# First unit of a retention and two-layer FFN kernel: the activation's sum kept in its PSUM bank, and five decoding operations issued earlier

## The chip, the cores and the metric

The kernel runs on one core of one Trainium2 chip. The time is the device time of one execution in microseconds; the median of several runs is compared.

## The reference, cut to what matters

```python
def reference(**kwargs):
    attn_out = _attn_ref(**attn_kwargs)              # retention: 4 batches, 8 heads, 768 steps, 64 per head
    x = attn_out.transpose(0, 2, 1, 3).reshape(B * S, H * D)     # 3072 tokens x 512
    x = _moe_ref(x=x, **moe_kwargs)
    return _moe2_ref(x=x, **moe2_kwargs)             # gated experts, one per token

def _moe_ref(x, w_in, w_out):
    h = x @ w_in                                     # 512 -> 2048
    g = np.maximum(h, 0.0) + np.log1p(np.exp(-np.abs(h)))
    return (g @ w_out).astype(np.float32)            # 2048 -> 512
```

The change lies in the second of the three parts, in the computation of `g`.

## The kernel before, in words

The 3072 tokens are worked on in 8 units of 384 tokens. Unit T of the feed-forward layer and the retention of unit T+1 run in one pipeline of 16 steps, one for each slice `f` of 128 of the 2048 hidden columns; steps are counted through, s = 16 T + f. Step s issues, in this order on each engine (the order is written out by hand in the loop over `s`, and each engine runs its queue in that order):

- a piece of the retention of the next unit (`attn_a`, `attn_m`: two small products and two masks `am`),
- `dec`: some operations of the decoding of the weights (below),
- `mm1(s)`, line 621: 12 matmuls of the first layer into a PSUM bank `hp`. These banks come from a pool of two, so the bank of step s is that of step s-2,
- in six steps of the first unit (2, 3, 5, 6, 8, 9) the transposes `tq` and their copy `kt` or `qt` on ScalarE (`attn_prep`, line 430),
- `act_a(s)` on ScalarE: `u` = |h| (line 632), `u` = exp(-u) (633), in the first unit `t` twice (635, 636), `ln` = log(1+u) (637), which with `t` makes a corrected log1p,
- the rest of the retention piece (`attn_b`: sums `y`, state update `wsb` on VectorE),
- `dec_fin`: for each decoded weight block the copy of its high half on ScalarE (line 340), the load of a further block, and its low half on GpSimd (342),
- `act_p(s)` on GpSimd (VectorE for the very first): two additions that finish `ln` (648, 649),
- `act_hi(s-1)`: the sum `g` on VectorE (659 in the first unit), then its rounded high half `hi` on ScalarE (660),
- one more decoding operation, then `act_lo(s-1)`: the low half `lo` = g - hi on VectorE (666), and `dec_fin` again,
- `mm2(s-2)`, line 678: 9 matmuls of the second layer with `hi` and `lo` of step s-2.

The matmuls run on operands split into a high and a low half, so every matrix product is made of three.

The weights of the feed-forward layer come as 64-bit floats. They are decoded during the first unit, in 32 blocks, each with three VectorE operations (lines 321, 325, 329: mask and shift, or, or), 96 in all; `dec(n)` issues the next n of them. 30 are issued in the opening before step 0, the rest in the steps: before the change 2 in step 0, one in step 1, and then by turns four and five a step up to step 15. A block `m` has two buffers.

The line of the loop that sets this, and the place of the sum:

```python
                dec(3+s%2 if s > 1 else (2, 0)[s])
                ...
                    dec(1 if s > 1 else 1)
```

After the feed-forward part come the gate, the sorting of tokens to experts and the experts' layers; they are untouched.

Of the kernel before, what the change touches and what calls it, by code (L numbers as in the profile page):

```python
# [7 lines left out]
F32 = mybir.dt.float32  # L8
# [4 lines left out]
ALU = mybir.AluOpType  # L13
# [8 lines left out]
TT = 384  # L22
# [53 lines left out]
def retention_moe_moe2(ctx: ExitStack, tc: tile.TileContext, a: dict, out: bass.AP):  # L76
    nc = tc.nc
# [200 lines left out]
    with tc.manual_schedule():  # L278
        with ExitStack() as p1:
# [5 lines left out]
            gp2 = p1.enter_context(tc.tile_pool(name="gp2", bufs=2))  # L285
# [58 lines left out]
            def dec(n):  # L344
                for _ in range(n):
                    next(steps, None)
# [60 lines left out]
            def attn_scale_q(U, p):  # L407
                if U < UN:
                    scale_nat(U, p, st[U, p]["qs"], qnat)
                    return  # L410
                qs = st[U, p]["qs"].rearrange("p (c j) -> p c j", j=32)
                r0 = U % 2 * (TT // 32)
                nc.gpsimd.tensor_tensor(
                    out=qs, in0=qs, in1=qtab[:, p, r0:r0 + TT // 32].unsqueeze(2).to_broadcast([128, TT // 32, 32]),
                    op=ALU.mult,
                )
# [17 lines left out]
            def attn_a(U, p, c, dst=None, am=None):  # L434
                s = st[U, p]
                cs = slice(c * 128, (c + 1) * 128)
                if dst is None:
                    sc = ps_s.tile([128, 512], F32, name="sc")
                    dst = (sc[:, 0:128], wps[:, 256:384])
                    am = at1.tile([128, 256], F32, name="am")  # L440
                for h in range(2):
                    hs = slice(h * 64, (h + 1) * 64)
                    nc.tensor.matmul(dst[h], lhsT=s["kt"][hs, cs], rhs=s["qt"][hs, cs], start=True, stop=True)  # L443
                s["am", c] = am, dst

            def attn_m(U, p, c):
                s = st[U, p]
                am, dst = s["am", c]
                for h in range(2):
                    i = nc.vector.tensor_tensor(out=am[:, h * 128:(h + 1) * 128], in0=dst[h], in1=mask, op=ALU.mult)  # L450
                return i
# [44 lines left out]
            def attn_first(U, i):  # L496
                if i == 0:
                    attn_load_qk(U, 0)
                    attn_load_v(U, 0)
                    attn_load_k(U, 0)  # L500
                elif i == 1:
                    attn_scale_q(U, 0)
                    attn_scale_v(U, 0)
                elif i == 2:
                    attn_prep(U, 0, 0)
                elif i == 3:
                    attn_prep(U, 0, 1)
                    attn_load_qk(U, 1)
                    attn_load_v(U, 1)

            def attn_ahead(U, i):
                p, c = seq[i]
                if c == 0 and p + 1 < NP:
                    attn_prep(U, p + 1, 0)
                if c == 1 and p + 1 < NP:
                    attn_prep(U, p + 1, 1)
# [99 lines left out]
            def mm1(T, f):  # L616
                hp = ps_h.tile([128, 512], F32, name="hp")[:, 0:TT]
                n = 0
                for w, x in ((0, xth[T]), (1, xth[T]), (0, xtl[T])):
                    for kk in range(KD):  # L620
                        nc.tensor.matmul(  # L621
                            hp, lhsT=wi[:, f, w, kk, :], rhs=x[:, kk, :], start=(n == 0), stop=(n == 3 * KD - 1),
                        )
                        n += 1
                gl[T, f] = hp

            def act_a(T, f):
                hp = gl[T, f]
                u = gp2.tile([128, TT], F32, name="u")
                ln = gp2.tile([128, TT], F32, name="ln")  # L630
                t = at1.tile([128, TT], F32, name="t")
                nc.scalar.activation(out=u, in_=hp, func=AF.Abs)  # L632
                nc.scalar.activation(out=u, in_=u, func=AF.Exp, scale=-1.0)  # L633
                if T == 0:
                    nc.scalar.activation(out=t, in_=u, func=AF.Identity, bias=1.0)
                    nc.scalar.activation(out=t, in_=t, func=AF.Identity, bias=io8[:, 7:8])
                nc.scalar.activation(out=ln, in_=u, func=AF.Ln, bias=1.0)  # L637
                g = gp2.tile([128, TT], F32, name="g")
                if T:
                    nc.scalar.activation(out=g, in_=hp, func=AF.Relu)  # L640
                gl[T, f] = u, ln, t, g, hp
# [10 lines left out]
            def act_hi(T, f):  # L652
                g, ln, hp = gl[T, f]
                hi = gp3.tile([128, TT], F32R, name="hi")
                gl[T, f] = g, ln
                if T:
                    nc.vector.tensor_tensor(out=g, in0=g, in1=ln, op=ALU.add)  # L657
                else:
                    nc.vector.scalar_tensor_tensor(out=g, in0=hp, scalar=0.0, in1=ln, op0=ALU.max, op1=ALU.add)  # L659
                nc.scalar.activation(out=hi, in_=g, func=AF.Copy)  # L660
                gh[T, f] = hi

# [146 lines left out]
            def init_records():  # L809
                rec0 = mp.tile([128, RW, 2], I32, name="rec0", tag="m")  # L810
                nc.gpsimd.memset(rec0, 0)
                nc.gpsimd.memset(rec0[:, :, 0:1], BIG)
                nc.sync.dma_start(
                    out=recd.rearrange("(p n) two -> p (n two)", p=128), in_=rec0.rearrange("p n two -> p (n two)"),
                )
# [14 lines left out]
            def zero(tiles):  # L830
                for t in tiles:
                    nc.scalar.activation(
                        out=t.rearrange("p (k t) -> p k t", k=KD), in_=ident.unsqueeze(1).to_broadcast([128, KD, 128]), func=AF.Copy, scale=0.0,
                    )
# [16 lines left out]
            for s in range(NS + 2):  # L851
                T, f = divmod(s, NF)
                U = T + 1
                i = f - 2 if U < NU and 2 <= f < 2 + len(seq) else None
                if f >= 14 and U + 1 < NU:
                    attn_first(U + 1, f - 14)
                if s == 2 * NF:
                    init_records()
                if s == 1:
                    attn_a(U, *seq[0])  # L860
                    attn_m(U, *seq[0])
                if i is not None:
                    if s != 2:
                        attn_a(U, *seq[i])
                        attn_m(U, *seq[i])
                    if i % CPU == 0 and i + CPU < len(seq):
                        attn_scale_q(U, i // CPU + 1)
                dec(3+s%2 if s > 1 else (2, 0)[s])
                if s < NS:
                    mm1(T, f)  # L870
                for fn in todo.get(s + 0.5, []):
                    fn()
                if f < 2 and 1 < U < NU:
                    attn_first(U, 2 + f)
                if i is not None:
                    attn_ahead(U, i)
                if s < NS:
                    act_a(T, f)
                if i is not None:
                    attn_b(U, *seq[i])  # L880
                dec_fin()
                if s < NS:
                    act_p(T, f)
                if s == NS:
                    hp2.extend(
                        pool.tile([128, GRP], F32, name=f"hp2_{i}", tag=tag)
                        for i, (pool, tag) in enumerate(((ps_s, "wps"), (ps_s, "y"), (ps_h, "hp"), (ps_h, "hp")))
                    )
                    lg = ps_s.tile([128, 512], F32, name="lg", tag="sc")
                    zero([lg])  # L890
                if 1 <= s <= NS:
                    act_hi(*divmod(s - 1, NF))
                    dec(1 if s > 1 else 1)
                    act_lo(*divmod(s - 1, NF))
                dec_fin()
                if i is not None:
                    attn_third(U, i)
                if s >= 2:
                    mm2(*divmod(s - 2, NF))
                if f == 1 and T > 0:  # L900
                    x1_out(T - 1)
                for fn in todo.get(s, []):
                    fn()
                if s == NS:
                    begin()
# [16 lines left out]
        with ExitStack() as left:  # L922
# [194 lines left out]
            for m, (ns, nb) in enumerate(PAIRS):  # L1117
                s, b = vis[ns], vis[nb]
# [48 lines left out]
            with tc.For_i(0, nv, 1) as it:  # L1167
                s = {"n": 0, "nb": 4, "xg": xgb[0]}
# [39 lines left out]
```

## Time and profile before

| | us |
|---|---|
| median of 3 runs | 1016.39 (1016.14 to 1019.01) |
| profiled execution, its own time | 1017.94 |
| span of its trace | 1016.1 |
| TensorE busy in the span | 962.1 (95%) |
| VectorE busy | 589.9 (58%) |
| ScalarE busy | 492.1 (48%) |
| GpSimd busy | 562.1 (55%) |

The shares are means over stages of different kinds. The slices of the span (a digit is the busy share of a fortieth in tenths) show which engine is full in which stage. The first unit takes from about 44 to 154 us. In the views, PE is TensorE, DVE is VectorE, ACT is ScalarE, POOL is GpSimd; "L659" is line 659 of the kernel. A row of the timeline gives start, duration, engine, line, operation, output and input, and in brackets the engine's idle time before it with what released it. Rows that follow each other on one engine overlap a little, so the distance of two starts is the better measure of what an operation costs in a row.

### The profile page before, as it was taken

The page shows a single profiled execution, that of the slowest core. Times are in us where ns is not written, and L with a number is a line of the kernel's source. Part 1 is how long each engine was busy: PE and PEld are TensorE (multiplying, and loading weights), DVE is VectorE, ACT ScalarE, POOL GpSimd, SP SyncE. Part 2 cuts the span into 40 slices and gives each one's busy share as a digit, 9 for nine tenths or more (in the row PEclk, how much of TensorE's full clock was granted, in tenths as well). Part 3 has the DMA queues.
Part 4 walks back from the last instruction along what each step waited for, and adds up shares of the span by engine and source line. Part 5 has one row for each costly group of instructions (what it writes and reads, how often), then busy time and mean ns, then how long its engine had stood idle before and what let it go on. Part 6 is the DMA issues. An engine that isn't in the chain of part 4 may idle for free.

```text
span 1016.1 us, 16219 instructions
## 1 busy us (share of the span) xinstructions
PE 962.1 (95%) x5666; PEld 801.4 (79%) x5666; DVE 589.9 (58%) x1292; ACT 492.1 (48%) x947; POOL 562.1 (55%) x457
## 2 busy tenths in 40 slices
PE   7798989999999999999999999999797999999994
PEld 6676768888888888888888888888685878798883
DVE  6799995546444654644564464446335375556743
ACT  3556555445445544544554454455453365354650
POOL 5577776446554653654564465446562673546642
PEclk9999999999999999999999999999897999999998
DMA  9744334123320412321041232001027394557710
GB/s 229 193 127 129 123 94 117 33 40 90 63 39 9 120 30 40 96 54 32 13 121 25 40 100 49 9 2 63 1 86 267 95 340 149 202 173 239 251 54 21
DMA packets 180692, 100.46 MB, mean 99 GB/s; under 512 B 140594, under 2 KB 159186, under 8 KB 180608
## 3 DMA queue, kind: packets, MB, share of 16 engines
q1 hardware_dynamic: 176032, 89.56, 32.0%
q0 software_dynamic: 4144, 9.04, 2.6%
q8 instruction: 46, 0.75, 0.3%
q10 hardware_dynamic: 432, 0.79, 0.2%
q14 instruction: 38, 0.31, 0.1%
HBM read 83.43 MB, written 17.85 MB: 100 GB/s over the span
## 4 chain that ended last, share of the span: by engine, by line
PE 72%; DVE 15%; issue 4%; ACT 4%; POOL 2%; DMA 2%; SPq 0%; DVEq 0%; POOLq 0%; ACTq 0%
PE hp L621 21%; PE ac L678 21%; PE op L1007 9%; PE hp L967 9%; DVE m L325 3%; PE sc L443 3%; PE y L465 3%; DVE lo L666 3%; PE hp L981 2%; DVE m L329 2%; DVE m L321 1%; PE y L463 1%; PE tp L703 1%; PE hp L179 1%; ACT hi L660 1%
## 5 line engine op out<-in xcount | busy, mean ns | idle before, releaser
L648 POOL TENSOR_TENSOR ln<-ln,t 128x384 f32<-128x384 f32 x127 | 151.3, 1191 | 260.0 <-ACT ln L637 234.5
L678 PE MATMUL ac<-wo,hi 128*128 128x512 f32 x768 | 272.4, 409 | 6.1 <-ACT hi L660 6.1
L621 PE MATMUL hp<-xth,wi 128*128 128x384 f32 x1024 | 214.8, 352 | 10.9 <-DVE g L659 10.0
L621 PEld LDWEIGHTS hp<-xth,wi 128*128 128x128 f32 x1024 | 177.7, 190 | 25.3 <-DVE g L659 11.8
L678 PEld LDWEIGHTS ac<-wo,hi 128*128 128x128 f32 x768 | 145.0, 189 | 43.4 <-ACT hi L660 7.2
L632 ACT ACTIVATE u<-hp 128x384 f32<-128x384 f32 x128 | 62.7, 490 | 240.0 <-PE hp L621 226.0
L649 POOL TENSOR_TENSOR ln<-ln,u 128x384 f32<-128x384 f32 x127 | 153.0, 1205 | 10.0
L678 PE MATMUL ac<-wo,lo 128*128 128x512 f32 x384 | 152.3, 397 | 1.1 <-DVE lo L666 0.6
L666 DVE TENSOR_TENSOR lo<-g,hi 128x384 fp32r<-128x384 f32 x128 | 97.6, 763 | 69.7 <-ACT hi L660 69.7
L621 PE MATMUL hp<-xtl,wi 128*128 128x384 f32 x512 | 110.6, 337 | 0.0
L163 POOL TENSOR_TENSOR l<-raw,h 128x1024 fp32r<-128x1024 f32 x30 | 77.1, 2580 | 54.8 <-ACT h L160 32.6
L646 DVE TENSOR_SCALAR t<-u 128x384 f32<-128x384 f32 x112 | 41.8, 373 | 95.7 <-ACT u L633 93.5
L621 PEld LDWEIGHTS hp<-xtl,wi 128*128 128x128 f32 x512 | 91.8, 190 | 0.0
L678 PEld LDWEIGHTS ac<-wo,lo 128*128 128x128 f32 x384 | 72.8, 190 | 16.3 <-DVE lo L666 4.8
L163 DVE TENSOR_TENSOR l<-raw,h 128x1024 fp32r<-128x1024 f32 x42 | 77.0, 1860 | 14.4 <-ACT h L160 14.4
L660 ACT ACTIVATE hi<-g 128x384 fp32r<-128x384 f32 x128 | 67.2, 525 | 28.6 <-DVE g L657 20.3
L482 DVE TENSOR_TENSOR wsb<-wps,wsb 64x64 f32<-64x64 f32 x112 | 24.7, 220 | 94.5 <-PE wps L474 93.8
L160 ACT ACTIVATE h<-raw 128x1024 fp32r<-128x1024 f32 x71 | 72.8, 1057 | 9.9 <-PE hp L981 3.7
L633 ACT ACTIVATE u<-u 128x384 f32<-128x384 f32 x128 | 67.2, 525 | 4.1
L637 ACT ACTIVATE ln<-u 128x384 f32<-128x384 f32 x128 | 67.1, 524 | 3.5
L657 DVE TENSOR_TENSOR g<-g,ln 128x384 f32<-128x384 f32 x112 | 61.7, 551 | 0.9 <-POOL ln L649 0.9
L1007 PE MATMUL op<-h,gh 128*128 128x512 f32 x152 | 60.0, 394 | 0.0
(218 smaller groups left out, 1578.6 us busy)
## 6 DMA issues: line engine op xcount, KB each, us to landing
raw<-in_moe_w SPq DMA_DIRECT2D x72, 512.0 KB, 5.1
raw<-in_moe_w_in SPq DMA_DIRECT2D x16, 512.0 KB, 4.0
raw<-in_moe_w_out SPq DMA_DIRECT2D x16, 512.0 KB, 3.5
kn<-in_k SPq DMA_DIRECT2D x56, 96.0 KB, 2.5
vn<-in_v SPq DMA_DIRECT2D x56, 96.0 KB, 2.6
x1d<-x SPq DMA_DIRECT2D x21, 256.0 KB, 3.1
out<-x SPq DMA_DIRECT2D x21, 256.0 KB, 3.3
ks<-in_k SPq DMA_DIRECT2D x96, 48.0 KB, 2.4
```

Source lines behind the costliest of these rows:

```text
L160: nc.scalar.activation(out=h, in_=r, func=AF.Copy)
L163: eng.tensor_tensor(out=lo, in0=r, in1=h.bitcast(F32), op=ALU.subtract)
L621: nc.tensor.matmul(hp, lhsT=wi[:, f, w, kk, :], rhs=x[:, kk, :], start=(n == 0), stop=(n == 3 * KD - 1),)
L633: nc.scalar.activation(out=u, in_=u, func=AF.Exp, scale=-1.0)
L637: nc.scalar.activation(out=ln, in_=u, func=AF.Ln, bias=1.0)
L648: eng.tensor_tensor(out=ln, in0=ln, in1=t, op=ALU.subtract)
L649: eng.tensor_tensor(out=ln, in0=ln, in1=u, op=ALU.add)
L660: nc.scalar.activation(out=hi, in_=g, func=AF.Copy)
L666: nc.vector.tensor_tensor(out=lo, in0=g, in1=gh[T, f].bitcast(F32), op=ALU.subtract)
L678: nc.tensor.matmul(ac[T, j], lhsT=x[:, js], rhs=wo[:, f, w, :], start=(f == 0 and n == 0), stop=(f == NF - 1 and n == 2),)
L967: nc.tensor.matmul(hp2[(2 * i + g) % 4][:, 0:w], lhsT=wt[:, kk, g * 128:(g + 1) * 128], rhs=x[:, kk, 0:w], start=(n == 0 and kk == 0), sto ...
L1007: nc.tensor.matmul(op, lhsT=s[x][:, f, js], rhs=s[w, f // 2][:, f % 2, :], start=(f == 0 and n == 0), stop=(f == NF2 - 1 and n == 2),)
```

## The change

In the first unit (`T` = 0) no separate buffer holds the sum `g`: VectorE writes it back into the bank `hp` that it read, and both `hi` (ScalarE) and `lo` (VectorE) read it from there. Only the units after the first keep the buffer in SBUF. Besides, step 0 issues five decoding operations ahead instead of two, and step 1 two instead of none; the steps from 2 on are issued the same numbers, so the decoding ends with step 14 instead of 15.

```diff
@@ -635,7 +635,7 @@
                 nc.scalar.activation(out=ln, in_=u, func=AF.Ln, bias=1.0)
-                g = gp2.tile([128, TT], F32, name="g")
+                g = gp2.tile([128, TT], F32, name="g") if T else hp
                 if T:
                     nc.scalar.activation(out=g, in_=hp, func=AF.Relu)
                 gl[T, f] = u, ln, t, g, hp
@@ -656,7 +656,7 @@
                 if T:
                     nc.vector.tensor_tensor(out=g, in0=g, in1=ln, op=ALU.add)
                 else:
-                    nc.vector.scalar_tensor_tensor(out=g, in0=hp, scalar=0.0, in1=ln, op0=ALU.max, op1=ALU.add)
+                    nc.vector.scalar_tensor_tensor(out=g, in0=g, scalar=0.0, in1=ln, op0=ALU.max, op1=ALU.add)
                 nc.scalar.activation(out=hi, in_=g, func=AF.Copy)
                 gh[T, f] = hi
@@ -865,7 +865,7 @@
-                dec(3+s%2 if s > 1 else (2, 0)[s])
+                dec(3+s%2 if s > 1 else (5, 2)[s])
                 if s < NS:
                     mm1(T, f)
```

VectorE's queue in steps 0 and 1, from the first operation of a decoded block to `lo` of step 0; `am` are the masks, `m` the decoded block, L648 and L649 finish `ln` of step 0. Before:

```order
L321 TENSOR_SCALAR m<-raw 128x512
L325 SCALAR_TENSOR_TENSOR m<-raw,m 128x512
L648 TENSOR_TENSOR ln<-ln,t 128x384
L649 TENSOR_TENSOR ln<-ln,u 128x384
L450 TENSOR_TENSOR am<-sc,cst 128x128
L450 TENSOR_TENSOR am<-wps,cst 128x128
L659 SCALAR_TENSOR_TENSOR g<-hp,ln 128x384
L329 SCALAR_TENSOR_TENSOR m<-raw,m 128x512
L666 TENSOR_TENSOR lo<-g,hi 128x384
```

The same place in the changed kernel, from the three operations added in step 0 on:

```order
L329 SCALAR_TENSOR_TENSOR m<-raw,m 128x512
L321 TENSOR_SCALAR m<-raw 128x512
L325 SCALAR_TENSOR_TENSOR m<-raw,m 128x512
L648 TENSOR_TENSOR ln<-ln,t 128x384
L649 TENSOR_TENSOR ln<-ln,u 128x384
L450 TENSOR_TENSOR am<-sc,cst 128x128
L450 TENSOR_TENSOR am<-wps,cst 128x128
L329 SCALAR_TENSOR_TENSOR m<-raw,m 128x512
L321 TENSOR_SCALAR m<-raw 128x512
L659 SCALAR_TENSOR_TENSOR hp<-hp,ln 128x384
L325 SCALAR_TENSOR_TENSOR m<-raw,m 128x512
L666 TENSOR_TENSOR lo<-hp,hi 128x384
```

Three operations more stand ahead of L648, and two more between the masks and the sum; the sum now goes to `hp`, and `lo` reads `hp`.

ScalarE's queue in the changed kernel, from the end of one step's chain to the end of the next one's, in the middle of the first unit (`wi` and `wo` are decoded blocks' high halves):

```order
L637 ACTIVATE ln<-u 128x384
L340 ACTIVATE wi<-m 128x512
L660 ACTIVATE hi<-hp 128x384
L340 ACTIVATE wo<-m 128x512
L632 ACTIVATE u<-hp 128x384
L633 ACTIVATE u<-u 128x384
L635 ACTIVATE t<-u 128x384
L636 ACTIVATE t<-t,cst 128x384
L637 ACTIVATE ln<-u 128x384
L340 ACTIVATE wi<-m 128x512
L660 ACTIVATE hi<-hp 128x384
```

Before, the row of `hi` read `hi<-g`; its place behind the chain of the following step is the same. In every step up to 14 exactly one block's copy stands between `ln` and `hi`; in step 15 none does any more.

VectorE's queue at the end of the first unit, from the decoding of step 15 to the first transpose for the next unit. Before:

```order
L325 SCALAR_TENSOR_TENSOR m<-raw,m 128x512
L329 SCALAR_TENSOR_TENSOR m<-raw,m 128x512
L321 TENSOR_SCALAR m<-raw 128x512
L325 SCALAR_TENSOR_TENSOR m<-raw,m 128x512
L659 SCALAR_TENSOR_TENSOR g<-hp,ln 128x384
L329 SCALAR_TENSOR_TENSOR m<-raw,m 128x512
L666 TENSOR_TENSOR lo<-g,hi 128x384
L432 STREAM_TRANSPOSE kt<-ks 128x384
```

And in the changed kernel, with step 14's end ahead of it:

```order
L659 SCALAR_TENSOR_TENSOR hp<-hp,ln 128x384
L329 SCALAR_TENSOR_TENSOR m<-raw,m 128x512
L666 TENSOR_TENSOR lo<-hp,hi 128x384
L659 SCALAR_TENSOR_TENSOR hp<-hp,ln 128x384
L666 TENSOR_TENSOR lo<-hp,hi 128x384
L432 STREAM_TRANSPOSE kt<-ks 128x384
```

The five operations of step 15 are gone: its sum follows `lo` of the step before directly.

## Rows read from the trace of the kernel before

**Rows 1.** The page's slices of the span, 40 of 25.4 us.
```profile
DVE  6799995546444654644564464446335375556743
PEclk9999999999999999999999999999897999999998
```
**Rows 2.** Busy time by stretch: length, PE, PEld, DVE, ACT, POOL, clock, DMA share, GB/s.
```profile
175.00:200.00 25.00, 25.00 (x153) 20.34 (x152) 13.88 (x37) 10.95 (x23) 13.82 (x13) 1.00 0.23 45
```
**Rows 3.** Timeline, steps 15 to 17: first-layer matmuls, ScalarE's `u` and `hi`.
```profile
142.25 2.44 PE L621 MATMUL hp<-xth,wi 128*128 128x384 f32 x8 [2.03 <-DVE g L659]
...
149.64 1.66 PE L621 MATMUL hp<-xth,wi 128*128 128x384 f32 x8 [1.43 <-DVE g L659]
...
154.52 1.57 PE L621 MATMUL hp<-xth,wi 128*128 128x384 f32 x8
...
146.07 0.49 ACT L632 ACTIVATE u<-hp 128x384 f32<-128x384 f32 x1 [3.35 <-PE hp L621]
...
152.09 0.49 ACT L632 ACTIVATE u<-hp 128x384 f32<-128x384 f32 x1 [0.20 <-PE hp L621]
...
154.11 0.53 ACT L660 ACTIVATE hi<-g 128x384 fp32r<-128x384 f32 x1
```
**Rows 4.** Timeline of TensorE: the first-layer matmuls of steps 2 and 3.
```profile
50.37 2.73 PE L621 MATMUL hp<-xth,wi 128*128 128x384 f32 x8 [2.62 <-DVE g L659]
...
57.95 1.68 PE L621 MATMUL hp<-xth,wi 128*128 128x384 f32 x8
```
**Rows 5.** Busy time by stretch, from step 2's first-layer matmuls to step 15's.
```profile
50.37:142.25 91.88, 81.30 (x439) 64.64 (x440) 88.09 (x127) 55.58 (x111) 67.29 (x51) 0.98 0.44 127
```
**Rows 6.** By line, 50 to 152 us: count, ns min/median/max, first and last start.
```profile
L666 DVE TENSOR_TENSOR lo<-g,hi x15: 1056/1366/1372, 51.3 to 151.1; 128x384 fp32r<-128x384 f32 x15
...
L490 DVE TENSOR_TENSOR xtl<-y,xth x4: 543/544/546, 74.2 to 138.0; 128x384 fp32r<-128x384 f32 x4
```
**Rows 7.** Timeline of VectorE: `lo` of step 15, after the decoding.
```profile
154.67 0.56 DVE L666 TENSOR_TENSOR lo<-g,hi 128x384 fp32r<-128x384 f32 x1 [0.59 <-ACT hi L660]
```
**Rows 8.** Timeline of VectorE, steps 0 to 2.
```profile
45.42 0.69 DVE L325 SCALAR_TENSOR_TENSOR m<-raw,m 128x512 int32<-128x512 int32 x1
48.30 0.56 DVE L648 TENSOR_TENSOR ln<-ln,t 128x384 f32<-128x384 f32 x1 [2.18 <-ACT ln L637]
...
49.77 0.55 DVE L659 SCALAR_TENSOR_TENSOR g<-hp,ln 128x384 f32<-128x384 f32 x1
...
58.73 1.33 DVE L666 TENSOR_TENSOR lo<-g,hi 128x384 fp32r<-128x384 f32 x1 [1.05 <-ACT hi L660]
```
**Rows 9.** Timeline, step 7: first-layer matmuls, and ScalarE's first operation behind them.
```profile
87.00 1.68 PE L621 MATMUL hp<-xth,wi 128*128 128x384 f32 x8
...
89.47 0.49 ACT L632 ACTIVATE u<-hp 128x384 f32<-128x384 f32 x1 [1.97 <-PE hp L621]
```
**Rows 10.** Timeline of ScalarE, step 2: first `u`, the block's copy, `hi`.
```profile
55.04 0.48 ACT L632 ACTIVATE u<-hp 128x384 f32<-128x384 f32 x1
...
57.67 0.61 ACT L340 ACTIVATE wo<-m 128x512 fp32r<-128x512 f32 x1
58.19 0.51 ACT L660 ACTIVATE hi<-g 128x384 fp32r<-128x384 f32 x1
```
**Rows 11.** Timeline, step 9, which prepares the next head pair: matmuls, ScalarE's `u`.
```profile
101.52 1.66 PE L621 MATMUL hp<-xth,wi 128*128 128x384 f32 x8
...
104.63 0.49 ACT L632 ACTIVATE u<-hp 128x384 f32<-128x384 f32 x1
```
**Rows 12.** By line, 50 to 152 us, as rows 6: the three decoding operations.
```profile
L321 DVE TENSOR_SCALAR m<-raw x21: 410/420/1427, 52.2 to 146.8; 128x512 int32<-128x512 int32 x21
...
L325 DVE SCALAR_TENSOR_TENSOR m<-raw,m x21: 676/1099/1672, 53.5 to 147.9; 128x512 int32<-128x512 int32 x21
...
L329 DVE SCALAR_TENSOR_TENSOR m<-raw,m x22: 682/1338/1719, 50.2 to 149.5; 128x512 int32<-128x512 int32 x22
```
**Rows 13.** Timeline of GpSimd: the low half of the block decoded before step 0.
```profile
45.79 1.48 POOL L342 TENSOR_TENSOR wo<-m,wo 128x512 fp32r<-128x512 f32 x1 [2.15 <-ACT wo L340]
```

## Prediction

> **What bounds the kernel now.** I read the slices of the span first. In the slices of the first unit (about 44 to 154 us) VectorE is the engine at nine tenths, and the TensorE clock dips twice [rows 1]. Later the roles change: from 175 to 200 us TensorE is busy 25.00 of 25.00 us [rows 2]. So a microsecond lost or won in the first unit arrives at the end of the kernel unchanged, because behind it stands only TensorE work without gaps. The whole question is when the first-layer matmuls of step 17 (second unit, second step) start: 154.52 us now [rows 3].
>
> Inside the first unit I looked at where the step s starts its first-layer matmuls, which I call M(s): M(2) = 50.37, M(3) = 57.95, M(15) = 142.25, M(16) = 149.64, M(17) = 154.52 [rows 3, 4]. Between M(2) and M(15), 13 steps, VectorE is busy 88.09 of 91.88 us [rows 5]: its own sum sets the pace now. M(2) waited 2.62 us for the sum `g` of step 0, so the PSUM bank is already a link of the chain [rows 4].
>
> **What the change does to each operation.** The low half `lo` reads its first input from PSUM instead of SBUF. It takes 1.366 us in the median of 15 now; the nearest row is the same operation in the same shape with one PSUM input, the split of the attention output, 0.544 us in the same stretch, narrowly spread although GpSimd works beside it [rows 6]. I take 0.54, 0.82 less. The upper end is no gain. Alone, behind the decoding, `lo` from SBUF takes 0.56 us [rows 7], so PSUM as a source costs nothing here. [...] Writing `g` to PSUM is not shown in the trace; I take its 0.55 us as it is [rows 8], with zero to 0.1 us more per step as bounds. The high half `hi` on ScalarE, now read from PSUM, is taken unchanged.
>
> The wait is the other side. The first-layer bank has two buffers, so M(s) waits until the bank of step s-2 was read for the last time. That was `g`; now it is `lo`. Between the two stand, on VectorE, one decoding operation, and on ScalarE the copy `hi`. And `hi` of step s-1 is queued on ScalarE behind the whole chain of step s (`u`, `u`, `t`, `t`, `ln`) and one decoded block's copy. That chain reads the matmuls of step s. So a **ring** closes, one turn per step: `lo`(s-2) frees the bank, the matmuls M(s) run, ScalarE does its chain, the block copy, `hi`(s-1), then `lo`(s-1), which frees the next bank. Before, `g` did not wait for `hi`, and the ring was open.
>
> **The price of one turn**, from starts of instructions: VectorE's last reader to M, 0.60 (49.77 to 50.37) [rows 4, 8]; M to `u`, 2.47 (87.00 to 89.47) [rows 9]; `u` to the block copy, 2.63, copy to `hi`, 0.52 (55.04, 57.67, 58.19) [rows 10]; `hi` to `lo`, 0.54 (58.19 to 58.73) [rows 8, 10]. Sum 6.76 us. In steps that prepare the next head pair (s = 2, 3, 5, 6, 8, 9) the transposes and one more ScalarE copy stand between M and `u`: 3.11 (101.52 to 104.63) [rows 11], so 7.40 us. A turn at the low clock, as at M(2): M to `u` 4.67, sum 8.96 [rows 4, 10].
>
> VectorE's own sum falls to (88.09 - 13 x 0.82) / 13 = 5.96 us a step [rows 5, 6]. Steps alternate between four and five decoding operations, about 0.95 us each (mean of the three medians [rows 12]), so 5.5 and 6.4 us: below the ring in every step. What `lo` saves on VectorE becomes waiting.
>
> **The start.** Three of the five moved decoding operations go ahead of the sum of step 0, into a pause: VectorE ends at 46.11 and continues at 48.30 [rows 8]. L329 runs there beside a GpSimd operation until 47.27 [rows 13], so 1.34, then 0.42 and 0.69 [rows 12]: end 48.55, 0.25 too late. Then as now 1.47 us until the place of `g` (48.30 to 49.77), 50.0; but there the other two (1.34 and 0.42) come first: `g` at 51.8. Behind it 0.55 and one more operation, 1.10, then `lo` at 53.4, and 0.60 later M(2) = **54.0**, 3.6 later than now. With the shortest durations of these rows it is 52.7, with the longest 55.4.
>
> **The sum.** M(2) 54.0. Step 2 at the low clock, since TensorE idles longer before it than now: 8.96. Steps 3 to 14: 5 x 7.40 + 7 x 6.76 = 84.3 (now 84.3: by chance the same). Step 15 has no decoding any more, its five operations went to the start, so no block copy: 6.24; but TensorE waits about 2 us before it, as at 142.25, where 2.03 us of waiting went with the low clock and M to `u` took 3.82 instead of 2.47 [rows 3, 9]: 7.59. Step 16 is of the second unit, its ScalarE chain 2.02 (152.09 to 154.11) [rows 3]: 0.60 + 2.47 + 2.02 + 0.54 = 5.63. M(17) = 54.0 + 8.96 + 84.3 + 7.59 + 5.63 = 160.5, against 154.52: **6.0 us later**. By the profiled execution, 1017.94 + 6.0 = 1023.9; that one lies 1.55 above the median of the runs, so 1016.4 + 6.0 = **1022.4 us**. What is late next: behind M(17) nothing waits for VectorE, so the loss stays.
>
> Lower end of this case: M(2) at 52.7, full clock in steps 2 and 15 (7.40 and 6.24): 156.3, 1.8 us later, 1018.2. Upper end: M(2) at 55.4, 0.1 us for `g` in each of 15 steps, one more low-clock turn (1.35): 164.7, 10.2 later, 1026.6.
>
> **Rivals.**
> *VectorE's sum stays the pace, and the kernel is faster.* Place: steps 2 to 16. If the turn is shorter than VectorE's 5.5 to 6.4 us, 15 x 0.82 = 12.3 us are won, and the five operations leave step 15 (4.8 us), less the 3.6 at the start: 13.5 faster, 1003. It decides when a turn falls below about 6.4 us, that is 0.4 below mine. For it: VectorE is the full engine now. Against it: every link of the ring is a row, and they add up to the observed 58.73 at step 2.
> *The two cancel.* The ring's links overlap a little (ScalarE starts on the bank before I think, or the decoding hides wholly in the start) and the clock stays up: the lower end above less 0.1 a step, 1016.7. For it: steps 3 to 14 come out equal anyway.
> *More low clock.* With a pause of TensorE in each turn, the low clock could hold in four more turns, 1.35 each: 5.4 more, 1028. Before, pauses of 1.43 us passed without it [rows 3], and TensorE's mean pause from M(2) to M(15), (91.88 - 81.30) / 13 = 0.81 us [rows 5], stays as it is where the steps keep their length; that speaks against it. [...]
> *`lo` does not get faster*, since `hi` still comes from SBUF beside GpSimd: each turn 0.82 longer, 15 turns, 12.3 more: 1035. The attention's split speaks against it.
>
> **Chances.** Forecast 0.60 (up to its bounds, 1019.4 to 1026.6); faster by VectorE's sum, wholly or in part, 0.11; cancelled 0.15; more low clock 0.10; no gain in `lo` 0.04. A measurement of this kernel can tell about 0.3%, 3 us, from no change. So faster 0.11, same 0.15, slower 0.74. The range 1015 to 1029 leaves out the first and the last rival and a little of the edges.
>
> **What the changed profile would show.** M(2) near 54 with a wait on `lo`, at the low clock; first-layer matmuls waiting for L666 instead of L659 in every step, starts some 6.8 and 7.4 us apart; `lo` at 0.55 us; VectorE no longer full in the first unit, waiting for `hi`; M(17) near 160. The forecast is wrong if M(3) to M(15) takes under 80 us, or if M(2) is below 52.

## The result and the profile after

The change makes the kernel slower: 1029.87 us median of 4 runs (1027.13 to 1030.99), against 1016.62 (1016.14 to 1019.01) for the kernel before on the same chip. The ratio is 1.0122 [1.0096, 1.0148], 12 us; the medians lie 13.25 us apart. The profiled execution took 1030.41 us, its span is 1028.6. The forecast had the sign and the ring, but only about half of the size (1022.4), and 1029.87 lies just outside its range.

First the page of the changed kernel: its slices and the group of the first-layer matmuls (busy us, mean ns, idle time before with what ended most of it).

```profile
DVE  5888884545644654554475464545435375556743
PEclk9989999999999999999999999999897999999998
...
L621 PE MATMUL hp<-xth,wi 128*128 128x384 f32 x1024 | 217.9, 355 | 28.3 <-DVE lo L666 28.1
```

VectorE stands at eight tenths in the first unit where it stood at nine [rows 1], so it now waits for something; and of the 28.3 us that TensorE waits ahead of a first-layer matmul, 28.1 are ended by `lo`. Busy time by stretch, with the columns of [rows 2]:

```profile
54.91:156.71 101.80, 81.56 (x440) 67.66 (x440) 83.02 (x126) 52.85 (x108) 65.06 (x52) 0.93 0.39 112
...
87.31:89.90 2.59, 2.59 (x8) 2.59 (x9) 2.56 (x5) 0.00 (x0) 1.72 (x2) 0.50 0.23 57
...
156.71:158.30 1.59, 1.59 (x9) 1.59 (x10) 0.00 (x0) 0.00 (x0) 1.51 (x3) 1.00 0.00 0
175.00:200.00 25.00, 25.00 (x151) 20.32 (x151) 13.44 (x37) 12.25 (x26) 12.32 (x12) 1.00 0.40 93
```

The first row answers to [rows 5]: from M(2) to M(15) the same work takes 101.80 us instead of 91.88, VectorE is busy 83.02 of them instead of 88.09 of 91.88, and the mean granted clock fell from 0.98 to 0.93. The last row answers to [rows 2]: later, TensorE is as full as before. From M(17) to the end of the span it is 861.2 us here and 861.6 before (1028.6 - 167.40 and 1016.1 - 154.52), so the whole loss lies ahead of M(17). The line of `lo`, 50 to 168 us, with what it waits for and who waits for it (us, times); this answers to [rows 6]:

```profile
L666 DVE TENSOR_TENSOR lo<-hp,hi x16: 544/558/559, 54.3 to 167.9; 128x384 fp32r<-128x384 f32 x16
...
  ACT hi L660: 12.9, 9
...
  PEld hp L621: 31.8, 15
```

The first-layer matmuls, one row for a step (M(2), then M(4) to M(8), M(15) to M(17)), answer to [rows 3, 4]:

```profile
54.91 2.93 PE L621 MATMUL hp<-xth,wi 128*128 128x384 f32 x8 [6.10 <-DVE lo L666]
...
71.83 1.66 PE L621 MATMUL hp<-xth,wi 128*128 128x384 f32 x8 [1.29 <-DVE lo L666]
...
78.55 1.66 PE L621 MATMUL hp<-xth,wi 128*128 128x384 f32 x8 [1.09 <-DVE lo L666]
...
87.31 2.93 PE L621 MATMUL hp<-xth,wi 128*128 128x384 f32 x8 [2.16 <-DVE lo L666]
...
96.06 1.66 PE L621 MATMUL hp<-xth,wi 128*128 128x384 f32 x8 [1.29 <-DVE lo L666]
...
104.17 2.93 PE L621 MATMUL hp<-xth,wi 128*128 128x384 f32 x8 [2.48 <-DVE lo L666]
...
156.71 1.66 PE L621 MATMUL hp<-xth,wi 128*128 128x384 f32 x8 [2.28 <-DVE lo L666]
...
162.91 1.66 PE L621 MATMUL hp<-xth,wi 128*128 128x384 f32 x8 [1.76 <-DVE lo L666]
...
167.40 1.66 PE L621 MATMUL hp<-xth,wi 128*128 128x384 f32 x8
```

Two things are to be seen. All first-layer matmuls from M(2) to M(16) wait for `lo`, and M(4) to M(5) is 6.72 us, M(7) less M(6) 8.75. And three steps besides step 2 run their eight matmuls in 2.93 us instead of 1.66, at a granted clock of 0.50 instead of 1.00: those of M(6), M(8) and M(12), behind pauses of 2.16, 2.48 and 2.17 us.

The table sets the distance from M(1) to M(17) apart, for every kernel of this study, from the starts in its timeline. The opening ahead of M(1) varies by an execution (44.9 to 46.4 us) and has nothing to do with the change. Each row is a single execution. The last one, of a kernel whose median equals that of the kernel before, has a sum 1.5 us lower, so differences of that size between two rows tell nothing by themselves.

| kernel | M(1) to M(2) | step 2 | steps 3 to 14 | step 15 | step 16 | sum |
|---|---|---|---|---|---|---|
| before | 5.00 | 7.58 | 84.30 | 7.39 | 4.88 | 109.15 |
| forecast for the change | 8.63 | 8.96 | 84.3 | 7.59 | 5.63 | 115.1 |
| the change | 8.48 | 9.53 | 92.27 | 6.20 | 4.49 | 120.97 |
| sum only (e1) | 6.42 | 9.53 | 84.08 | 7.64 | 4.48 | 112.15 |
| decoding only (e2) | 7.37 | 8.31 | 84.95 | 4.72 | 4.51 | 109.86 |
| longer hold only (e3) | 7.05 | 9.80 | 100.99 | 9.41 | 5.93 | 133.18 |
| change + filling (e4) | 8.51 | 7.37 | 88.14 | 6.22 | 4.50 | 114.74 |
| change, one operation more (e5) | 9.77 | 9.53 | 85.03 | 6.20 | 4.51 | 115.04 |
| change, three fewer (e6) | 7.21 | 9.53 | 92.68 | 6.71 | 4.49 | 120.62 |
| e1, `hi` early (e7) | 6.10 | 8.75 | 89.85 | 7.20 | 4.49 | 116.39 |
| e7 + filling (e8) | 6.10 | 6.71 | 89.77 | 7.08 | 4.48 | 114.14 |
| e1, `hi` mid (e9) | 6.42 | 9.01 | 90.13 | 7.10 | 4.49 | 117.15 |
| e9 + filling (e10) | 6.45 | 6.87 | 89.41 | 7.76 | 4.48 | 114.97 |
| before + filling (e11) | 5.00 | 7.06 | 83.67 | 7.43 | 4.48 | 107.64 |

So of the 11.8 us that the change loses here, 8.0 are lost in steps 3 to 14, where the forecast had none.

### The profile page after: what moved, and what is told of

Same layout as the page of the kernel before. It is cut to its first block, busy times and chain, and to the rows that moved or that the text cites. A ratio compares the mean times of both kernels' runs of the same rounds, so it can differ in the third digit from the quotient of the medians.

```text
span 1028.6 us, 16218 instructions
## 1 busy us (share of the span) xinstructions
PE 960.0 (93%) x5666; PEld 802.1 (78%) x5666; DVE 582.5 (57%) x1292; ACT 489.4 (48%) x947; POOL 558.3 (54%) x457
## 4 chain that ended last, share of the span: by engine, by line
PE 74%; DVE 10%; ACT 6%; issue 4%; POOL 2%; DMA 2%; SPq 1%; DVEq 0%; POOLq 0%; ACTq 0%
PE hp L621 24%; PE ac L678 20%; PE op L1007 9%; PE hp L967 8%; PE sc L443 3%; PE y L465 3%; DVE m L325 2%; PE hp L981 2%; PE y L463 1%; DVE lo L666 1%; DVE m L321 1%; ACT u L633 1%; PE tp L703 1%; DVE m L329 1%; ACT u L632 1%
## 5 line engine op out<-in xcount | busy, mean ns | idle before, releaser
L648 POOL TENSOR_TENSOR ln<-ln,t 128x384 f32<-128x384 f32 x127 | 148.8, 1172 | 260.1 <-ACT ln L637 235.0
L621 PE MATMUL hp<-xth,wi 128*128 128x384 f32 x1024 | 217.9, 355 | 28.3 <-DVE lo L666 28.1
L621 PEld LDWEIGHTS hp<-xth,wi 128*128 128x128 f32 x1024 | 180.1, 193 | 43.2 <-DVE lo L666 31.8
L649 POOL TENSOR_TENSOR ln<-ln,u 128x384 f32<-128x384 f32 x127 | 150.5, 1185 | 9.9
L666 DVE TENSOR_TENSOR lo<-g,hi 128x384 fp32r<-128x384 f32 x112 | 77.1, 688 | 66.3 <-ACT hi L660 66.3
L660 ACT ACTIVATE hi<-g 128x384 fp32r<-128x384 f32 x112 | 58.9, 526 | 24.1 <-DVE g L657 20.9
L657 DVE TENSOR_TENSOR g<-g,ln 128x384 f32<-128x384 f32 x112 | 61.7, 551 | 0.9 <-POOL ln L649 0.9
```

The source lines that it names most:

```text
L621: nc.tensor.matmul(hp, lhsT=wi[:, f, w, kk, :], rhs=x[:, kk, :], start=(n == 0), stop=(n == 3 * KD - 1),)
L648: eng.tensor_tensor(out=ln, in0=ln, in1=t, op=ALU.subtract)
L649: eng.tensor_tensor(out=ln, in0=ln, in1=u, op=ALU.add)
L666: nc.vector.tensor_tensor(out=lo, in0=g, in1=gh[T, f].bitcast(F32), op=ALU.subtract)
```

## The experiments

Where it says "filling", matmuls of ones are added whose product nobody reads. Each ratio is to the kernel before on the same chip.

**e1, the sum in the bank without the moved decoding** (against the changed kernel):

```diff
-                dec(3+s%2 if s > 1 else (5, 2)[s])
+                dec(3+s%2 if s > 1 else (2, 0)[s])
```

> The sum in the bank, the decoding as before the change (2 and 0 operations in steps 0 and 1). Theory A (the ring: the bank is free only after lo, and hi stands on ScalarE behind the next step's chain): M(2) comes about 2.5 us earlier than in the changed kernel, since only L329 stands between g and lo, but still waits for lo; the turns stay 6.7 and 7.4 us with some of 8 to 9, and step 15 has its decoding again and so about 0.5 us more: 1027 to 1030 us, most of the loss there. Rival B (the five moved operations are the loss, the sum in the bank costs nothing): 1016 to 1018 us.

Measured: 1021.03 us (9 runs, 1018.10 to 1023.25) against 1016.73, ratio 1.0045 [1.0032, 1.0058]. Neither range holds that. The ring is there: every turn from step 3 to 14 is 7.37 or 7.38, or 6.71 to 6.92 where no head pair is prepared, with a wait for `lo` ahead of each, and their sum, 84.08, is the forecast's 84.3. But the kernel loses only about 4 us, a third of what the change costs, and by the table not in these steps: 1.4 us are the later M(2), which now waits for `lo`, and 1.95 are step 2, a whole ring at the low clock (its eight matmuls in 2.93 us; 9.53 for 7.58). The closed ring alone doesn't explain steps 3 to 14 of the change.

**e2, the moved decoding without the sum in the bank** (against the changed kernel):

```diff
-                g = gp2.tile([128, TT], F32, name="g") if T else hp
+                g = gp2.tile([128, TT], F32, name="g")
...
-                    nc.vector.scalar_tensor_tensor(out=g, in0=g, scalar=0.0, in1=ln, op0=ALU.max, op1=ALU.add)
+                    nc.vector.scalar_tensor_tensor(out=g, in0=hp, scalar=0.0, in1=ln, op0=ALU.max, op1=ALU.add)
```

> The decoding as in the change (5 and 2), the sum in its own SBUF buffer. Theory A: the first-layer matmuls wait for g again; M(2) comes some 2 us later than before the change, step 15 has no decoding and gives 2 to 3 us back: 1014 to 1018 us. Rival B: the loss is here, 1024 to 1030 us.

Measured: 1017.71 us (10 runs) against 1016.73, ratio 1.0009 [0.9998, 1.0020]: no difference that can be told. What is lost at the start (2.4 us to M(2)) comes back in step 15, which has no decoding any more (4.72 instead of 7.39). So the moved decoding costs something only together with the closed ring.

**e3, the longer hold alone**: the kernel before, with a small read of the bank behind `lo`, so that the bank is held as long as in the change while `lo` still reads `g` from SBUF (against the kernel before):

```diff
-                gl[T, f] = g, ln
+                gl[T, f] = g, ln, hp
...
-                g, _ = gl[T, f]
+                g, _, hp = gl[T, f]
...
+                if T == 0:
+                    nc.vector.tensor_copy(blk, hp[:, 0:E])
```

> The kernel before, with one small read of the bank (8 columns) by VectorE behind lo in the first unit: the bank is held as long as in the change, but g, hi and lo read and write SBUF as before. Theory A: the ring closes and lo takes 1.3 us in it, so each turn is about 0.9 us longer than in the changed kernel: 1030 to 1038 us, more than the change. Rival C (holding the bank is harmless, the loss comes from PSUM as the place of g: slower operations or collisions): 1016 to 1019 us, the small reads alone costing at most 16 x 0.1 us.

Measured: 1041.34 us (4 runs) against 1016.73, ratio 1.0246 [1.0225, 1.0268], above both of its ranges. VectorE's timeline at the end of step 5:

```profile
87.05 1.32 DVE L666 TENSOR_TENSOR lo<-g,hi 128x384 fp32r<-128x384 f32 x1 [0.71 <-ACT hi L660]
88.29 0.15 DVE L668 COPY blk<-hp 128x8 f32<-128x8 f32 x1
```

The added read itself takes 0.15 us and ends 0.07 us after `lo`. The hold is what costs 24.6 us: `lo`, still 1.32 us long, now stands in the ring. The turns that keep the full clock are 7.59 and 8.24 us, 0.87 longer than those of e1, which has the same decoding; that is 10.4 us in steps 3 to 14. The other 6.5 us by which these steps exceed e1's are longer turns, up to 9.8 us, in part at the low clock: the mean granted clock from M(2) to M(15) is 0.89 here. So against e1 this shows what the faster `lo` is worth in a closed ring; e3 also differs from e1 in the place of `g`.

**e4, the change with filling**, to take the low clock away:

```diff
+                if 1 <= s <= 14:
+                    fl = ps_a.tile([128, DM], F32, name="fl", tag="ac0") if s == 1 else wps
+                    for _ in range(80 if s == 1 else 12):
+                        nc.tensor.matmul(fl[:, 384:512], lhsT=ones, rhs=ones, start=True, stop=True)
```

> The changed kernel, with small matmuls of ones (80 in step 1, 12 at the end of each of steps 2 to 14) that fill TensorE's pauses in the first unit. Theory D (the part of the loss beyond the forecast is the low clock in steps 2, 6, 8 and 12, about 1.35 us each, and it comes from the pauses): all first-layer matmuls of the unit at the full clock, those four turns 1.3 to 1.5 us shorter, 1023 to 1026 us. Rival E (the long turns are long because of VectorE or the waits, and the clock only shows in them): no gain, 1029 to 1031 us, or more, because the filling delays the matmuls.

Measured: 1024.60 us (4 runs) against 1016.73, ratio 1.0091 [1.0063, 1.0119]. TensorE's timeline, M(2) and M(6), and the busy time by stretch from M(2) to M(16):

```profile
54.54 1.66 PE L621 MATMUL hp<-xth,wi 128*128 128x384 f32 x8 [1.65 <-DVE lo L666]
...
84.78 1.66 PE L621 MATMUL hp<-xth,wi 128*128 128x384 f32 x8 [1.40 <-DVE lo L666]
...
54.54:156.27 101.73, 88.25 (x617) 73.56 (x617) 83.97 (x129) 55.81 (x114) 71.12 (x58) 1.00 0.41 112
```

The clock is 1.00 throughout, and the turns of step 2, 6, 8 and 12, 9.53, 8.75, 8.85 and 8.06 us in the change, are 7.37, 7.37, 7.36 and 6.71. That is 6.4 us in the trace, 5.3 by the medians and 3.2 by the two ratios, whose intervals overlap. But the turns of steps 5, 7 and 11 stay: 8.76, 8.11, 8.12 us, 1.4 longer than the ring. They are not the clock's doing; the low clock came behind them.

**What makes turns 5, 7 and 11 long.** VectorE in step 7 and in step 13 of the changed kernel, whose rings are equally long, with ScalarE's `hi` and GpSimd beside (timeline):

```profile
99.10 1.67 DVE L329 SCALAR_TENSOR_TENSOR m<-raw,m 128x512 int32<-128x512 int32 x1
100.69 1.05 DVE L321 TENSOR_SCALAR m<-raw 128x512 int32<-128x512 int32 x1
101.68 0.55 DVE L659 SCALAR_TENSOR_TENSOR hp<-hp,ln 128x384 f32<-128x384 f32 x1
102.14 1.50 DVE L325 SCALAR_TENSOR_TENSOR m<-raw,m 128x512 int32<-128x512 int32 x1
103.57 0.55 DVE L666 TENSOR_TENSOR lo<-hp,hi 128x384 fp32r<-128x384 f32 x1
...
146.30 1.67 DVE L329 SCALAR_TENSOR_TENSOR m<-raw,m 128x512 int32<-128x512 int32 x1
147.90 0.41 DVE L321 TENSOR_SCALAR m<-raw 128x512 int32<-128x512 int32 x1
148.23 0.55 DVE L659 SCALAR_TENSOR_TENSOR hp<-hp,ln 128x384 f32<-128x384 f32 x1
148.70 0.68 DVE L325 SCALAR_TENSOR_TENSOR m<-raw,m 128x512 int32<-128x512 int32 x1
149.38 0.56 DVE L666 TENSOR_TENSOR lo<-hp,hi 128x384 fp32r<-128x384 f32 x1
...
102.26 0.49 ACT L660 ACTIVATE hi<-hp 128x384 fp32r<-128x384 f32 x1 [0.50 <-DVE hp L659]
...
98.47 1.75 POOL L342 TENSOR_TENSOR wo<-m,wo 128x512 fp32r<-128x512 f32 x1
100.19 1.28 POOL L402 TENSOR_TENSOR vn<-vn,cst 128x384 f32<-128x384 f32 x1
101.83 1.27 POOL L342 TENSOR_TENSOR wi<-m,wi 128x512 fp32r<-128x512 f32 x1 [0.37 <-ACT wi L340]
...
149.05 1.46 POOL L342 TENSOR_TENSOR wo<-m,wo 128x512 fp32r<-128x512 f32 x1 [1.62 <-ACT wo L340]
```

In both steps the first three decoding operations run beside GpSimd's additions and a block's low half, and are long, 1.21 to 1.67 us, where those with nothing on GpSimd beside them take 0.41 (L321) or 0.68 to 0.69 (L325, L329). In step 13 the rest is undisturbed, and VectorE just keeps up: `lo` follows without a wait. In step 7 GpSimd also scales a piece of the retention (L402) beside the second L321, which takes 1.05 us instead of 0.41; the sum comes late, `hi` waits 0.50 us for it, and the operation behind the sum now meets GpSimd's next low half and takes 1.50 instead of 0.68. Together that is the 1.4 us by which the turn is longer. In step 5 the same happens (L321 1.06, `hi` waits 0.34, L325 1.55); in step 11 it is `xtl` on VectorE, ahead of the decoding, that makes the sum late (`xtl` itself waits 0.34 us for ScalarE; `hi` waits 0.34, L325 takes 1.56).

Why only in the change? In e1 33 decoding operations have been issued before step 2, in the change 38. The operations come in threes, one block, so the ends of the blocks fall at another place: with 38, every even step ends two blocks, and GpSimd's work on the second one falls into the odd step, which has five decoding operations instead of four. That is a theory with a clean test: change the number issued ahead, once so that the ends move and once so that they stay.

**e5 and e6, the place of the blocks' ends.** e5 issues one operation more ahead (39, which leaves the same remainder of three as e1); e6 three fewer (35, the remainder of the change):

```diff
-                dec(3+s%2 if s > 1 else (5, 2)[s])
+                dec(3+s%2 if s > 1 else (5, 3)[s])
```
```diff
-                dec(3+s%2 if s > 1 else (5, 2)[s])
+                dec(3+s%2 if s > 1 else (4, 0)[s])
```

> The changed kernel with 5 and 3 decoding operations in steps 0 and 1, one more than the change, 8 steps of three with nothing over: the steps from 2 on begin with L321 (even) and L325 (odd), as with 2 and 0. Theory F (the long turns 5, 7 and 11 of the change come from the place of the block ends in the steps: with 38 operations before step 2 an even step ends two blocks, and GpSimd's low half of the second one falls into the odd step with its five decoding operations): those turns go back to 7.4 and 6.7 us, and most low-clock turns behind them go too, M(2) about 1 us later: 1020 to 1024 us. Rival G (each operation issued ahead costs): 1030 to 1033 us.

> The changed kernel with 4 and 0 decoding operations in steps 0 and 1: 35 before step 2, the same place of the block ends as in the change, with three operations fewer ahead. Theory F: the turns 5, 7 and 11 stay above 8 us, with the low clock behind them; M(2) about 2 us earlier than in the change: 1025 to 1029 us. Rival G: between the sum alone (1021) and the change (1030), 1022 to 1025 us, without turns above 7.5 us in steps 3 to 14.

Measured, against 1017.54: e5 1023.69 us (4 runs), 1.0061 [1.0044, 1.0078]; e6 1028.43 (4 runs), 1.0101 [1.0084, 1.0118]. With more work ahead of the sum, e5 is faster; its steps 3 to 14 take 85.03 us, without the three turns of 8.1 to 8.8, and with full clock behind step 2 (1.65 to 1.69 us for the eight matmuls). One other turn, step 12, is long there, 7.84: the operation behind its sum, L321, takes 1.51 us. With less work ahead, e6 has the long turns all again, 92.68. For these steps the place decides, not the number. A remainder of one was not run. The operation behind the sum of e5's step 12, with GpSimd beside, and then VectorE in step 7 of e1, which e5 repeats, to set beside the change's:

```profile
134.03 1.51 DVE L321 TENSOR_SCALAR m<-raw 128x512 int32<-128x512 int32 x1
133.99 1.26 POOL L342 TENSOR_TENSOR wi<-m,wi 128x512 fp32r<-128x512 f32 x1 [1.52 <-ACT wi L340]
...
93.97 1.21 DVE L325 SCALAR_TENSOR_TENSOR m<-raw,m 128x512 int32<-128x512 int32 x1
95.10 0.55 DVE L659 SCALAR_TENSOR_TENSOR hp<-hp,ln 128x384 f32<-128x384 f32 x1
95.57 0.68 DVE L329 SCALAR_TENSOR_TENSOR m<-raw,m 128x512 int32<-128x512 int32 x1
96.54 0.56 DVE L666 TENSOR_TENSOR lo<-hp,hi 128x384 fp32r<-128x384 f32 x1 [0.29 <-ACT hi L660]
```

In e1 the operation behind the sum is undisturbed and `lo` waits 0.29 us for `hi`: ScalarE's ring is the pace, VectorE is not.

**e7 and e9, a shorter ring.** If the ring were all, issuing `hi` of the step before earlier on ScalarE must gain. e7 puts it ahead of `ln` in the next step's chain, and with it the sum on VectorE ahead of the state update; e9 puts `hi` behind that chain and ahead of the block's copy (both against e1; the old place is left to the later units):

```diff
+                if T == 0 and f:
+                    act_hi(T, f - 1)
                 nc.scalar.activation(out=ln, in_=u, func=AF.Ln, bias=1.0)
```
```diff
+                if 1 <= s < NF:
+                    act_hi(T, f - 1)
```

> The sum in the bank with the decoding as before (2 and 0), and in steps 1 to 15 hi of step s-1 is issued on ScalarE ahead of ln of step s instead of behind ln and the block's copy; g goes ahead of the state update on VectorE with it. Theory A (the ring through hi sets the pace): each turn 0.95 us shorter by the rows until VectorE's sum of about 6 us is the bound, 12 turns, 5 to 11 us less than the sum alone: 1010 to 1016 us. Rival H (GpSimd or VectorE sets the pace as soon as the ring gives way): no better than the sum alone, 1018 to 1022 us.

> The sum in the bank with the decoding as before (2 and 0); in steps 1 to 15 hi is issued on ScalarE directly behind ln, ahead of the decoded blocks' copies, VectorE's order unchanged. Theory A: the block's copy leaves the ring, each turn that the ring sets is 0.52 us shorter: at most 7 us less than the sum alone, 1014 to 1019 us. Rival H (VectorE's contended decoding is already close behind the ring): most of it is not won, 1019 to 1023 us.

Measured: e7 1024.49 us (4 runs) against 1017.54, 1.0063 [1.0046, 1.0081]; e9 1025.35 (4 runs) against 1016.45, 1.0083 [1.0066, 1.0099]. Both miss: by the ratios they are 2 and 4 us slower than e1 (e7's interval overlaps that of e1, e9's does not), and their steps 3 to 14 take 90 us. One row of VectorE's timeline in e7, and two of VectorE's waits in e9 (us, times, longest):

```profile
69.73 1.22 DVE L321 TENSOR_SCALAR m<-raw 128x512 int32<-128x512 int32 x1 [0.79 <-POOL wi L342]
```
```profile
DVE m L321 <- POOL wo L342: 1.8, 2, 0.9
DVE m L321 <- POOL wi L342: 1.7, 2, 0.9
```

VectorE now waits for GpSimd to give back a decoded block's buffer, which it did neither in the kernel before nor in the change, and its decoding operations take 1.12 us in the mean of steps 2 to 14 (66.2 us for 59 in e7, against 58.4 for 59 before). `lo` waits for `hi` in only three steps of e7 and six of e9 (1.7 and 3.9 us in all), where it was thirteen in e1 (8.6 us). With the ring shortened VectorE and GpSimd are the pace in most steps, and they aren't faster than the ring.

**e8, e10 and e11, the same with filling, and the control:** filling as in e4 (44 matmuls in step 1; 12 in each of steps 2 to 14 in e8, 16 in step 14 alone in e10 and e11).

> The kernel of the run before (hi ahead of ln), with filling matmuls: 44 in step 1 and 12 at the end of each of steps 2 to 14. Theory D (low clock behind pauses): the two low-clock turns (steps 2 and 15) go, 2.5 to 3 us less than without filling, 1007 to 1013 us. If the turns are short enough that TensorE has no pauses, the filling only takes its time (0.7 us a step) and the kernel is slower than without it, by up to 5 us.

> The same with filling matmuls in steps 1 (44) and 14 (16) alone, ahead of the two turns that ran at the low clock with the sum alone. Theory D: these two turns at the full clock, 1.4 us each: 2 to 3 us less than without the filling.

> The kernel before, with the same filling in steps 1 and 14 alone. Theory D: the first-layer matmuls of steps 2 and 15 run at the full clock; step 2 was bound by the chain through them, so 1 to 1.6 us are won there, step 15 was bound by VectorE and gives little: 1014 to 1016 us. If VectorE alone sets the pace from step 2 on, no change: 1016 to 1017.5 us.

Measured: e8 1021.99 us (4 runs) against 1017.54, 1.0045 [1.0028, 1.0062]; e10 1023.57 (4 runs) against 1016.45, 1.0061 [1.0044, 1.0078]; e11 1016.54 (10 runs) against 1016.45, 0.9999 [0.9989, 1.0008]. By the medians filling gives e7 2.5 us and e9 1.8 (the intervals overlap), and the kernel before nothing that can be measured: its step 2 is 0.5 us shorter in the one trace, but the medians are equal. Steps 3 to 14 of e7 stay at 89.8 us with it, with each step's eight matmuls in 1.66 to 1.68 us, so the low clock is not what makes them long. e8 misses its expected level as e7 does, e10 gains a little under the 2 to 3 us expected, and e11 falls into the second of its ranges. No version with the sum in the bank beats the kernel before, and no experiment gave one that does.

## Why the prediction was half right

**The ring: right.** M(s) waits for `lo` in every step, and `lo` for ScalarE's `hi` nine times (12.9 us). One turn of step 4, in ScalarE's and VectorE's timeline:

```profile
74.28 0.49 ACT L632 ACTIVATE u<-hp 128x384 f32<-128x384 f32 x1 [3.09 <-PE hp L621]
...
76.92 0.61 ACT L340 ACTIVATE wo<-m 128x512 fp32r<-128x512 f32 x1
77.44 0.47 ACT L660 ACTIVATE hi<-hp 128x384 fp32r<-128x384 f32 x1
...
77.94 0.56 DVE L666 TENSOR_TENSOR lo<-hp,hi 128x384 fp32r<-128x384 f32 x1 [1.30 <-ACT hi L660]
```

From M(4) = 71.83: 2.45, 2.64, 0.52, 0.50, and 0.61 to M(5) = 78.55, 6.72 in all; forecast 2.47, 2.63, 0.52, 0.54, 0.60, 6.76. Turns that prepare a head pair take 7.36 to 7.39 (7.40). The price list was good to 0.04 us, and e1, where nothing else is the pace, takes 84.08 us for steps 3 to 14 (84.3).

**`lo`: right.** 0.558 us in the median (0.54). That the source is PSUM cost nothing here: 0.56 us is also what it took alone from SBUF [rows 7]. The 0.1 us a step that the upper end allows for writing `g` to PSUM was the author's estimate, and no run shows it: the sum took 0.566 us in the median of 16, 0.554 before. The rival "no gain in `lo`" falls; e3, with e1's decoding, shows its price, 1041 us.

**The start: right in its sum, by errors that cancel.** M(2) is 3.48 us later counted from M(1), forecast 3.6 (54.91 against 54.0 is for the most part the opening, 1.06 us later in this execution). The terms were not right. From L648 to the end of the masks it took 2.41 us (49.84 to 52.25) where 1.47 were reckoned "as now", since L649 now stood beside a low half on GpSimd:

```profile
50.42 1.50 DVE L649 TENSOR_TENSOR ln<-ln,u 128x384 f32<-128x384 f32 x1
...
49.89 1.62 POOL L342 TENSOR_TENSOR wi<-m,wi 128x512 fp32r<-128x512 f32 x1 [1.59 <-ACT wi L340]
```

The two decoding operations behind the masks took 0.93 us together instead of 1.76, and the one behind the sum 0.64 instead of 1.10. That the sum fits is luck.

**VectorE's sum: wrong; this is the step that failed.** It said: 5.96 us a step, "so 5.5 and 6.4 us: below the ring in every step". Measured is 83.02 / 13 = 6.39 us a step, and in steps 5, 7 and 11 VectorE is busy 8.27, 8.01 and 7.63 us, above their rings of 7.36 and 6.72:

```profile
78.50:87.25 8.75, 8.27 (x13) 0.98 0.41 129
...
96.01:104.12 8.11, 8.01 (x10) 0.99 0.59 165
127.04:135.16 8.12, 7.63 (x14) 0.97 0.34 116
```

(These are stretches from the end of one `lo` to the end of the next; the number behind the comma is VectorE's busy time.) `lo` did give back its part: 7.2 us in 13 steps instead of 17.3. But the decoding operations took 61.7 us for 58 instead of 58.4 for 59, 1.06 us each instead of 0.99, and L321, 0.420 us in the median before [rows 12], took 1.214: GpSimd's work, which had stood beside a long `lo`, now stood beside them. That alone is not the loss: e1, whose steps 3 to 14 keep to the ring, has 6.27 us a step (81.52 / 13), nearly as much. What failed is to price each step by the mean of a whole unit, which says nothing on a step in which all five operations are disturbed: 6.8 us for the five of step 7, where 5 x 0.95 = 4.8 was reckoned. The cost is 3 x 1.4 = 4.2 us directly.

**The low clock: wrong in extent.** It was a rival of 0.10 with four more turns and 5.4 us. It came in three (6, 8 and 12), each the turn behind one that VectorE made long (5, 7 and 11), and cost 1.4, 1.5 and 1.3 us, 4.2 together. The argument against it was that the pauses stay as they are where the steps keep their length; the steps didn't keep it. Where they did, in e1, none of steps 3 to 14 fell to the low clock (1.66 to 1.68 us for the eight matmuls). (The two dips that the prediction reads from [rows 1] are not to be seen there, where the PEclk digits fall below nine only from 711 us on; they show in the 2.73 and 2.44 us of M(2) and M(15) [rows 3, 4].) Steps 3 to 14 are then 84.0 + 4.2 + 4.2 = 92.4, measured 92.27.

**Steps 15 and 16: over-estimated, in sum by 2.5 us.** Step 15 was taken at the low clock, 7.59; it ran at full clock and took 6.20, the 6.24 of the ring without the block's copy. Step 16 was taken as a whole ring, 5.63; it took 4.49:

```profile
166.87 0.47 ACT L640 ACTIVATE g<-hp 128x384 f32<-128x384 f32 x1
...
167.91 0.56 DVE L666 TENSOR_TENSOR lo<-hp,hi 128x384 fp32r<-128x384 f32 x1 [0.56 <-ACT hi L660]
```

M(17) starts at 167.40, half a microsecond before that `lo`, the one of step 15. In the second unit ScalarE copies the bank out to SBUF in its own step (line 640), and M(17) starts 0.06 us after that copy ends: by these times it got the bank of step 16, which came free before that of step 15. The forecast had counted the banks strictly by turns.

**Step 2** took 0.57 more than forecast (9.53 for 8.96): the low clock lasted longer than in the step that was its pattern [rows 4, 10]. The eight matmuls took 2.93 us instead of 2.73, and from M to `u` it was 5.27 (54.91 to 60.18) instead of 4.67.

The sum: start -0.15, step 2 +0.57, steps 3 to 14 +7.97, step 15 -1.39, step 16 -1.14, against the forecast's 6.0: 11.8. The medians say 13.25; the rest is within what single executions differ by. By kernels it is: closed ring 3.0 us (e1 less before), six operations more issued ahead of step 2 2.9 (e5 less e1), the place of the blocks' ends with the low clock behind it 5.9 (change less e5). By the ratios, which rest on four to nine runs each, the same three are 4.6, 1.6 and 6.2 us; the place is the largest by both. What isn't settled: why a pause of 2.28 us ahead of M(15) left the clock up, where 2.16 and 2.17 were followed by the low one; in e1 the same 2.28 us ahead of M(15) was followed by eight matmuls in 2.00 us instead of 1.66 and four in 1.48 instead of 0.85.

## What to carry to other kernels

Writing a result back in place into an accumulation bank saves a buffer and may make one operation faster (here `lo`, from 1.366 to 0.558 us), but it moves the bank's last reader to the end of the chain: go once around from that reader to the next matmul and to the next reader, through every queue between, and compare the turn with each engine's own sum. Take that sum for each step apart and with the neighbours that it will have in that step; a mean over a stage hides the step that is full. And if work is handed out in groups of three across steps of four and five, the remainder that one starts with can decide which step meets whose contention, as it did here between two of the three: try all three.

## What the hardware showed that was not expected

The contention between VectorE and GpSimd did not go away when one operation left it. `lo`, with one input in PSUM, was 0.56 us even beside a low half on GpSimd (149.38 beside 149.05), but its neighbours, whose tensors are in SBUF, then met the same GpSimd work: L321 0.41 or 1.05 to 1.23 us, L325 0.68 or 1.37 to 1.56, while GpSimd's low half took 1.26 to 1.75. The long ones end a little behind the GpSimd operation that was running when they came. The L325 at 102.14 ends at 103.64, 0.54 us after the low half that was running when it came (101.83 to 103.10); the L321 at 100.69 ends 0.27 us after the scaling (L402) that ran until 101.47. It is so for every decoding operation of the change from M(2) to M(15) that took over 0.3 us more than its shortest: the 20 of L325 and L329 end 0.54 or 0.55 us, the 13 of L321 0.27 to 0.29 us after the GpSimd operation that was running at their start. So what such an operation cost here can be read from the order of the two queues: it is what was left of the other's time, and 0.3 or 0.55 us.

The clock: three of the four pauses of 2.1 to 2.5 us from M(6) to M(15) were followed by a granted clock of 0.50 over the 2.93 us of the eight matmuls, which cost 1.3 to 1.5 us a time in a stretch where TensorE was not even the pace, since the matmuls stand in the ring. Filling removed it wholly (e4, 1.00 from M(2) to M(16)); in the kernel before, where no ring closes, filling ahead of the two steps at the low clock was worth nothing (e11, 1016.54 against 1016.45 us, though their eight matmuls took 1.68 and 1.65 us instead of 2.73 and 2.44).
